# First chunk in halves, half of the attention output transposed by DMA, and a searched order, in a fused attention and gated feed-forward kernel

## The chip, the cores and the metric

The kernel runs on 1 core of a Trainium2 chip. The metric is the device time of one execution in microseconds (us). Every group of runs had the kernel before timed beside it on the same chip. A run is called slow when it is over 1.5% above the fastest of its kernel. "Profile" is one execution with the hardware profiler; its span is about 1.8 us shorter than the timed figure. "Granted clock" is the share of full speed that PE's clock had by the profile.

Engines: PE (matmul), DVE (vector), ACT (scalar), POOL and SP, which here mainly issue DMAs. Each engine works through its own list of instructions, in the order that the program fixed; semaphores join the lists. PE writes its results to banks of PSUM, and a bank must be read out by DVE or ACT before it is written again. In the profile's lines L1041 is line 1041 of the kernel file, SPq is SP issuing a DMA, and `ps` is a PSUM bank.

## The reference, cut to what matters

Four sequences of 768 tokens, 8 heads of 64. Heads 0, 2 and 6 see all earlier tokens, the others four sink tokens and a window of 64. The attention output, 3072 x 512, goes through a gated feed-forward block:

```python
x   = attention(q, k, v)                       # 3072 x 512
g   = x @ w_gate;  val = x @ w_val             # 512 -> 1536
ffn = (gelu(g) * val) @ w_out                  # 1536 -> 512
out = x + sigmoid(x @ w_res) * ffn
```

## The kernel before

It works in six chunks of 512 tokens, four tiles of 128 each. A builder in the kernel file writes tasks with priorities and assumed durations, simulates its own idea of the chip, and fixes the instruction list of every engine from it. The parts that the argument touches:

```python
P_ot = Pool(many("otile", 3, [128, D_MODEL], FP32))      # THREE output tiles
...
"gv": (4, one(6, 7, 5, 4, 3, 2))                         # four PSUM banks for gate and value results
...
# queries and keys, from the third chunk's loads on: transposed by DMA, issued from SP
t = G.add("sp", 1.3, ... dma_start(at(BB.qkt)..., sv(), transpose=True) ..., dma=0.6, name="dT")
...
# output of a chunk: four tiles
for lt in range(4):
    rb, sr, ot = Buf(P_ps, "out"), Buf(P_sr), Buf(P_ot)
    ...                                                  # 4 residual-gate and 12 output matmuls on PE
    t1 = G.add("dve", ..., "otile = (1 + tanh) * ffn", ..., name="gated")   # cut
    t2 = G.add("dve", ..., "otile += x", ..., name="add")                   # cut
    G.add("sp", 0.6, ... dma_start(out[r0:r0 + 128, w], at(ot)[:, w]) ..., dma=0.75, name="out")
...
for _ in range(360):                                     # blank matmuls where the builder sees PE idle,
    G.add("pe", 0.06, ... matmul(blank, blank) ..., 1e9, name="warm")       # until the first gate
```

A chunk has four output tiles and there are three buffers for them, so the fourth tile cannot be written by DVE before the first tile's store has landed. On SP the stores stand in one list with the transposes of queries and keys and with the copies of values that heads with a window need ("vs").

The softmax here doesn't subtract the row's maximum and nothing guards it: scores larger than these inputs give would overflow.

Of the kernel before, what the change touches and what calls it, by code (L numbers as in the profile page):

```python
# [36 lines left out]
ROWS_UNTIL = 2  # L37

VK = ((1, 4), (3, 4), (4, 5), (4, 7))

# [389 lines left out]
def build_kernel(nc, q, k, v, w_gate, w_val, w_out, w_res, out):  # L430
# [34 lines left out]
        "av1": (2, one(0, 1)), "av2": (1, [(0, 1)]), "av0": (3, [(0, 1), (6, 7), (2, 3)]),  # L465
        "sc": (2, [(2, 3), (4, 5)]), "scr": (3, one(5, 4, 3, 2)), "scr0": (3, one(6, 5, 4, 3, 2)),
        "gv": (4, one(6, 7, 5, 4, 3, 2)), "gv0": (4, one(6, 7, 5, 4)), "gv00": (2, one(6, 7)), "out": (2, one(6, 7)), "warm": (1, one(7, 5, 1)),
# [56 lines left out]
    def load_weights():  # L524
        for j in range(3):
            for nm, t, src in (("g", wg, w_gate), ("v", wv, w_val)):
                s = slice(j * 512, (j + 1) * 512)
                wtok[nm, j] = dma("pool", -20 + j, 2.6, (lambda t=t, s=s: lambda: t[:, :, s])(),
                                  src[:, s].rearrange("(ci p) f -> p ci f", p=128))
        wtok["r"] = dma("pool", -12, 2.6, lambda: wr[:, :, :], w_res.rearrange("(ci p) f -> p ci f", p=128))  # L530
        for j in range(4):
            s = slice(j * 3, (j + 1) * 3)
            wtok["o", j] = dma("pool", -11 + j, 1.95, (lambda s=s: lambda: wo[:, s, :])(),
                               w_out[j * 384:(j + 1) * 384, :].rearrange("(fi p) c -> p fi c", p=128))

# [14 lines left out]
    def values(b, a, z, base, each, on_engines=False):  # L550

        BB = batch(b)
        for i in range(a, z):
            BB.vtok[i] = dma("pool", base, 0.9, (lambda i=i: lambda: at(BB.v)[:, i, :, 0:DHEAD])(),
                             v[b, :, i * 128:(i + 1) * 128, :].rearrange("h p d -> p h d"), bufs=[BB.v])
            BB.vtok[i].late = 1.3
        if a == 0:

            def vk(on, j, h0, h1):
                def fn(e):  # L560
                    o = at(BB.vk)[32 * j:32 * j + N_SINK, 2 * j:2 * j + 2, :]
                    i_ = at(BB.v)[0:N_SINK, 0, h0:h1 + 1:h1 - h0, :]
                    return e.activation(out=o, in_=i_, func=AF.Copy) if on == "act" else e.tensor_copy(out=o, in_=i_)
                return fn
            BB.vktok = [G.flex({"dve": (0.3, vk("dve", j, *hs)), "act": (0.35, vk("act", j, *hs))},
                               [BB.vtok[0]], base + 1500, bufs=[BB.v, BB.vk], name="vk") for j, hs in enumerate(VK)]
            for t in BB.vktok:
                t.slack = 12.0 if b else 0.0
                if b == 0:
                    t.alts = {"dve": t.alts["dve"]}  # L570
        a_ = max(a, 1)
        if on_engines:
            ts = []
            for dst, src, off in ((0, 64, 1), (64, 0, 0)):
                def vs(on, dst=dst, src=src, off=off):
                    def fn(e):
                        o = at(BB.vs)[dst:dst + 64, a_ - 1:z - 1, :, :].rearrange("p i h d -> p (i h d)")
                        i_ = at(BB.v)[src:src + 64, a_ - off:z - off, :, :].rearrange("p i h d -> p (i h d)")
                        return e.activation(out=o, in_=i_, func=AF.Copy) if on == "act" else e.tensor_copy(out=o, in_=i_)
                    return fn  # L580
                n_ = (z - a_) * 520
                ts.append(G.flex({"dve": (c_dve(n_, 3.0, False), vs("dve")), "act": (c_act(n_), vs("act"))},
                                 [BB.vtok[i - off] for i in range(a_, z)], 130, bufs=[BB.v, BB.vs], name="vs"))
            for i in range(a_, z):
                BB.vstok[i] = ts
            late_copies.extend(ts)
            return
        cuts = range(a_, z) if each else [a_]
        for lo in cuts:
            hi = lo + 1 if each else z  # L590
            ts = []
            for dst, src, off in ((0, 64, 1), (64, 0, 0)):
                ts.append(G.add("sp", 1.2, (lambda lo=lo, hi=hi, dst=dst, src=src, off=off: lambda e: e.dma_start(
                    at(BB.vs)[dst:dst + 64, lo - 1:hi - 1, :, :].rearrange("p i h d -> p (i h d)"),
                    at(BB.v)[src:src + 64, lo - off:hi - off, :, :].rearrange("p i h d -> p (i h d)")))(),
                    [BB.vtok[i - off] for i in range(lo, hi)], base + 1, bufs=[BB.v, BB.vs], dma=0.15 * (hi - lo),
                    name="vs", grp=("vs", b, lo)))
            for i in range(lo, hi):
                BB.vstok[i] = ts

    def loads_rows(c, si, b, a, z):
# [18 lines left out]
        values(b, a, z, base + (10 if c == 0 else 8), False, c == 0)  # L620

        per = 1 if c == 0 or n == 4 else 2
        for k_ in range(0, NPAIR, per):
            ps_ = ORDER[k_:k_ + per]
            pr = 1000 * c - 492 + ps_[0] if c else 40 * k_ - 5
# [55 lines left out]
    def attention(c, segs, xbuf, xtbuf, xtoks, xttoks):  # L681
        tiles = [(b, i) for (b, a, z) in segs for i in range(a, z)]
        todo = []
        for k_, p in enumerate(ORDER):
            P = B()
            P.heads, P.p, P.c, P.pr = PAIRS[p], p, c, 1000 * c + 40 * k_
# [23 lines left out]
        sinks = sink_scores(c, [t for t in tiles if t[1] > 0], 1000 * c + 40 + 5)  # L710
        for t in ph(c, "sc")[:-1]:
# [11 lines left out]
        last, norms = None, []  # L723
        for P in todo:
# [3 lines left out]
            last, tn = weigh(P, tiles, sinks, xbuf, x16, xtoks, xdeps, last)  # L728
            if P.heads[0] % 2 == 1:
                for cb in (P.heads[0] // 2, P.heads[1] // 2):  # L730
                    to_features(c, cb, P.pr, x16, xdeps, xtbuf, xttoks)
# [5 lines left out]
            norms.append(tn)  # L737

# [87 lines left out]
    def sink_scores(c, need, pr):  # L826

        S = B()
        S.where, S.four, S.et = {}, {}, Buf(P_ek)
        scr = Buf(P_ps, "sc")  # L830
        for m, (b, i) in enumerate(need):
            for h in (1, 3, 5, 7):
                S.where[h, b, i] = m * 128
            S.where[4, b, i] = 512
# [3 lines left out]
        cols = (need + need[-1:])[0:4]  # L838
# [13 lines left out]
        for j, (b, i) in enumerate(cols):  # L852
            mms.append((j, batch(b), slice(0, 64), 1, 512, i * 128, 128))

        def sc(e):
# [7 lines left out]
        S.txs = [G.add("act", c_act(640), lambda e: e.activation(  # L863
            out=at(S.et)[:, 0:640], in_=at(scr)[:, 0:640], func=AF.Exp, scale=SM_SCALE),
            [ts], pr, bufs=[scr, S.et], fset="exp", name="expk")]
# [3 lines left out]
    def weigh(P, tiles, sinks, xbuf, x16, xtoks, xdeps, last):  # L869
        n = len(tiles)  # L870
        c, pr, heads = P.c, P.pr, P.heads
        av = Buf(P_ps, "av2" if c else "av0")
# [3 lines left out]
        def windows(xs, lts):  # L876
            def fn(e):
                r = []
                for x in xs:
                    for lt in lts:  # L880
                        b, i = tiles[lt]
                        o, w, BB, h = x * 512 + lt * 65, P.where[x, None, b, i], batch(b), heads[x]
                        for s in range(2):
# [3 lines left out]
                                              start=lt == 0, stop=(i == 0), skip_group_check=True))  # L887
# [3 lines left out]
        def keys(x, lt):  # L891
            def fn(e):
                b, i = tiles[lt]
                o = x * 512 + lt * 65
                return [e.matmul(at(av)[:, o:o + 65], lhsT=at(P.et)[:, P.where[x, kt, b, i]:P.where[x, kt, b, i] + 128],  # L895
                                 rhs=at(batch(b).v)[:, kt, heads[x], :], start=lt == 0 and kt == 0, stop=(kt == i),
# [3 lines left out]
        def sinkf(x, h):  # L900
            def fn(e):
                r = []
                for lt, (b, i) in enumerate(tiles):
                    if i == 0:
                        continue
                    o, ko = x * 512 + lt * 65, sinks.where[h, b, i]
# [25 lines left out]
        def avv(d0, d1):  # L932
            return at(av).rearrange("p (x w) -> p x w", x=2)[:, :, 0:n * 65].rearrange(
# [8 lines left out]
        xview = lambda: at(xbuf)[:, 0:n, :].rearrange("p i (y x d) -> p x i y d", x=2, d=128)[:, :, :, heads[0] // 4, half]  # L942
        direct = c == 0 or heads[0] % 2
        if direct:

            xdeps.append(G.add("dve", c_dve(2 * n * 64), lambda e: e.tensor_tensor(  # L946
                out=at(x16)[:, :, :, half], in0=avv(0, DHEAD), in1=scale(), op=ALU.mult), [t1], pr - 2.5, bufs=[av, rc, x16], name="norm16"))
        t2 = G.add("dve", c_dve(2 * n * 64), lambda e: e.tensor_tensor(  # L948
            out=xview(), in0=avv(0, DHEAD), in1=scale(), op=ALU.mult), [t1] + xdeps, pr - 2 + (200 if c == 0 and heads[0] else 0), bufs=[av, rc, xbuf], name="norm")
        for i in range(n):  # L950
            xtoks.setdefault(i, []).append(t2)
        if not direct:
            def cast(on):
                return lambda e: (e.activation(out=at(x16)[:, :, :, half], in_=xview(), func=AF.Copy) if on == "act" else
                                  e.tensor_copy(out=at(x16)[:, :, :, half], in_=xview()))
# [4 lines left out]
    def to_features(c, cb, pr, x16, xdeps, xtbuf, xttoks):  # L960
        n = 4
# [5 lines left out]
        def ev(on):  # L967
            def fn(e):
                o, i_ = at(xtbuf)[:, cb, 0:n * 128], at16(scr)[:, 0:n * 128]
# [7 lines left out]
    def gate_value(c, xtbuf, xttoks):  # L977
# [4 lines left out]
        for f in range(NF):  # L982
            pr = 1000 * c + 500 + f
            kind = "gv" if f > 1 else "gv0" if c or f else "gv00"
# [20 lines left out]
            toks.append(th)  # L1005
# [3 lines left out]
    def output(c, h, htoks, xbuf, xtoks, xtbuf, xttoks):  # L1009
        segs = [(b, t) for (b, a, z) in CHUNKS[c] for t in range(a, z)]  # L1010
        for lt in range(4):
# [14 lines left out]
            for w in ((slice(0, 256), slice(256, 512)) if last else (slice(0, 512),)):  # L1026
                fb = Buf(P_ps, "gv" if last else "out")
                n = w.stop - w.start
                for j in range(6):
# [3 lines left out]
                        [prev_t, wtok["o", j * 2 // 3], wtok["o", (2 * j + 1) // 3]] + htoks[2 * j:2 * j + 2], pr,  # L1033
# [22 lines left out]
    firsts = None  # L1056
    for t in late_copies:
        t.order += [x for d in (batches[0].ktok, batches[0].qtok) for (p, i), x in d.items() if i == 0]
    for c, segs in enumerate(CHUNKS):
        xbuf, xtbuf, xtoks, xttoks = Buf(P_x), Buf(P_xt), {}, []  # L1060
        attention(c, segs, xbuf, xtbuf, xtoks, xttoks)
        firsts = firsts or xttoks
        h, htoks = gate_value(c, xtbuf, xttoks)
# [3 lines left out]
    for c in range(len(CHUNKS)):  # L1067
        gv, gelu = ph(c, "gv"), ph(c, "gelu")
        for f, t in gv:
            t.order += ph(c, "sc") + (ph(c, "xT") if f > (1 if c else 0) else [])  # L1070
        for t in ph(c, "table"):
            t.order += ph(c, "exp") + ([x for _, x in firsts[:2]] if c == 0 else [])
# [6 lines left out]

    span = G.schedule()  # L1080
# [54 lines left out]
```

## Time and profile before

| | before |
|---|---|
| time, median (range), runs beside the change | 278.58 us (278.38 to 278.83, n = 4) |
| span in the profile, mean granted clock | 276.8 us, 1.00 |
| PE busy; idle after the opening | 98%; 1.4 us |
| landing of the first chunk's output stores | 6.6 to 7.4 us |

The lines that carry the bound are in the prediction. One view which I did not read before predicting matters most now: SP's own list between the first and the second chunk's output. The columns are start, time to the end of the group, what it issues, and how many.

```profile
52.77 0.38 SPq L1041 DMA_DIRECT2D out_dram<-otile  x1
...
56.86 13.20 SPq L669 DMA_TRANSPOSE qkt<-qks  x8
...
70.80 15.03 SPq L669 DMA_TRANSPOSE qkt<-qks  x8
85.87 1.64 SPq L1041 DMA_DIRECT2D out_dram<-otile  x3
```

The reader is to see that the first chunk's first store leaves at 52.77 and the other three only at 85.87, behind sixteen transposes whose issue takes 13.20 + 15.03 us. By DVE's list the data of these three were complete at 56.6, 63.3 and 66.5, so three of four stores already wait 20 to 29 us in this kernel. PE shows no wait from it (its longest after the opening is 0.7 us): the store that frees the buffer went ahead.

### The profile page before, as it was taken

Reading aid. Unit: us, or ns where it says so; the run is one execution under the profiler, and the core shown is the slowest. Engines: PE = TensorE matmul, PEld = TensorE weight load, DVE = VectorE, ACT = ScalarE, POOL = GpSimd, SP = SyncE. Lnnn points to the kernel's source line nnn. Section 1 sums busy time; section 2 is a strip of 40 time slices with the busy share of each in tenths; the row PEclk is TensorE's granted clock in tenths of the full one; section 3 lists DMA queues with packets and bytes.
Section 4 is the critical chain, followed back from the end, with each engine's and each line's share of the span. In section 5 each row is a group of like instructions: output and inputs, shape, how many; then the busy total and the mean of one; then the engine's idle time right before and its main releaser. Section 6 shows DMA issues by size and latency. Waiting matters only on the chain.

```text
span 276.8 us, 5687 instructions
## 1 busy us (share of the span) xinstructions
PE 270.3 (98%) x2407; PEld 138.9 (50%) x2407; DVE 143.0 (52%) x260; ACT 137.5 (50%) x199; POOL 86.2 (31%) x120
## 2 busy tenths in 40 slices
PE   7999999999899999999999999999999999999995
PEld 7775454455444456444455444456444455544443
DVE  2696342477433467534377533366633258633234
ACT  3655366673433966334773333766233777333210
POOL 8999249991491613991000000000000000000000
PEclk9999999999999999999999999999999999999999
DMA  6999999999999999999711100021100011200022
GB/s 88 165 203 207 185 206 177 151 194 133 176 131 154 247 138 201 158 155 125 191 41 73 44 0 2 0 76 41 40 0 0 2 41 38 78 2 0 0 76 78
DMA packets 92474, 27.81 MB, mean 100 GB/s; under 512 B 81184, under 2 KB 88864, under 8 KB 92448
## 3 DMA queue, kind: packets, MB, share of 16 engines
q0 software_dynamic: 70320, 14.69, 66.8%
q1 hardware_dynamic: 22128, 12.76, 23.7%
q8 instruction: 19, 0.31, 0.5%
q14 instruction: 7, 0.06, 0.1%
HBM read 29.36 MB, written 6.29 MB: 129 GB/s over the span
## 4 chain that ended last, share of the span: by engine, by line
PE 95%; DVE 2%; DMA 2%; issue 1%; ACT 0%; POOLq 0%
PE ps L988 45%; PE ps L1031 23%; PE ps L1016 7%; PE ps L768 5%; PE ps L895 3%; PE ps L1047 3%; PE ps L885 2%; PE ps L963 2%; PE ps L631 2%; DMA qks<-in_q_dram 2%; PE ps L909 1%; PE ps L856 1%; ACT xT L970 0%; DVE otile L1035 0%; DVE x L946 0%
## 5 line engine op out<-in xcount | busy, mean ns | idle before, releaser
L1002 DVE SCALAR_TENSOR_TENSOR hT<-gact,ps 128x512 f16<-128x512 f16 x72 | 49.5, 687 | 70.5 <-ACT gact L1000 70.5
L988 PE MATMUL ps<-xT,wg 128*128 128x512 f16 x288 | 85.2, 379 | 0.5 <-ACT xT L970 0.5
L988 PE MATMUL ps<-xT,wv 128*128 128x512 f16 x288 | 85.2, 379 | 0.0
L1000 ACT ACTIVATE gact<-ps 128x512 f16<-128x512 f32 x72 | 43.0, 597 | 78.2 <-PE ps L988 78.2
L1031 PE MATMUL ps<-wo,hT 128*128 128x512 f16 (+1 forms) x300 | 71.6, 371 | 0.2
L988 PEld LDWEIGHTS ps<-xT,wv 128*128 128x128 f16 x288 | 28.1, 98 | 33.8
L988 PEld LDWEIGHTS ps<-xT,wg 128*128 128x128 f16 x288 | 27.7, 98 | 33.7 <-ACT xT L970 0.6
L784 ACT ACTIVATE er<-ps 128x1024 f16<-128x1024 f32 (+3 forms) x40 | 34.5, 904 | 14.4 <-PE ps L768 14.4
L1031 PEld LDWEIGHTS ps<-wo,hT 128*128 128x128 f16 x300 | 25.8, 98 | 28.4 <-DVE otile L1035 3.7
L520 POOL DMA_DIRECT2D qks<-in_k_dram x36 | 28.4, 831 | 31.8 <-DMA qkt<-qks 22.8
L1035 DVE SCALAR_TENSOR_TENSOR otile<-srs,ps 128x512 f32<-128x512 f32 (+1 forms) x25 | 16.6, 664 | 26.4 <-PE ps L1031 26.4
L520 POOL DMA_DIRECT2D qks<-in_q_dram x36 | 28.9, 851 | 0.8 <-POOLq L1117 0.8
L1016 PE MATMUL ps<-wr,xT 128*128 128x512 f16 x96 | 24.7, 380 | 0.0
L520 POOL DMA_DIRECT2D va<-in_v_dram x24 | 21.4, 943 | 6.4 <-PE ps L909 6.4
L1019 ACT ACTIVATE srs<-ps 128x512 f32<-128x512 f32 x24 | 14.4, 598 | 12.4 <-PE ps L1016 12.0
L768 PE MATMUL ps<-qkt 64*128 64x64 f16 (+4 forms) x396 | 17.2, 215 | 0.0
L1038 DVE TENSOR_TENSOR otile<-otile,xtok 128x512 f32<-128x512 f32 (+1 forms) x25 | 16.5, 661 | 0.5
L948 DVE TENSOR_TENSOR xtok<-ps,rcp 128x512 f32<-128x512 f32 x24 | 16.3, 686 | 0.3
L768 PEld LDWEIGHTS ps<-qkt 64*128 64x128 f16 x396 | 10.3, 94 | 8.2 <-issue 3.4
L784 ACT ACTIVATE es<-ps 128x1024 f16<-128x1024 f32 x12 | 12.2, 1020 | 3.5 <-PE ps L768 3.5
L1016 PEld LDWEIGHTS ps<-wr,xT 128*128 128x128 f16 x96 | 8.7, 98 | 10.4 <-ACT gact L1000 0.5
L970 ACT ACTIVATE xT<-ps 128x512 f16<-128x512 f16 x11 | 6.3, 596 | 15.2 <-PE ps L963 15.2
(58 smaller groups left out, 197.0 us busy)
## 6 DMA issues: line engine op xcount, KB each, us to landing
out_dram<-otile SPq DMA_DIRECT2D x23, 256.0 KB, 2.5
va<-in_v_dram POOLq DMA_DIRECT2D x24, 128.0 KB, 17.7
qks<-in_k_dram POOLq DMA_DIRECT2D x32, 64.0 KB, 16.3
qks<-in_q_dram POOLq DMA_DIRECT2D x32, 64.0 KB, 16.9
wg<-in_moe_w_gate_dram POOLq DMA_DIRECT2D x3, 512.0 KB, 10.0
wv<-in_moe_w_val_dram POOLq DMA_DIRECT2D x3, 512.0 KB, 12.4
wo<-in_moe_w_out_dram POOLq DMA_DIRECT2D x4, 384.0 KB, 22.4
vs<-va SPq DMA_DIRECT2D x4, 260.0 KB, 5.8
```

What stands on the lines that cost most here:

```text
L520: return G.add(eng, issue, lambda e: e.dma_start(out_ap(), in_ap), deps, prio, bufs=bufs, dma=cost, name=name, grp=grp)
L768: return [e.matmul(at(scr)[:, oo:oo + w], lhsT=at(BB.qkt)[half, 1, p, k0:k0 + 128], rhs=at(BB.qkt)[half, 0, p, qq:qq + w], start=True, sto ...
L784: return e.activation(out=o, in_=i_, func=AF.Exp, scale=SM_SCALE)
L948: t2 = G.add("dve", c_dve(2 * n * 64), lambda e: e.tensor_tensor(out=xview(), in0=avv(0, DHEAD), in1=scale(), op=ALU.mult), [t1] + xdeps, ...
L988: return lambda e: [e.matmul(at(dst)[:, :], lhsT=w[:, ci, f * 128:(f + 1) * 128], rhs=at(xtbuf)[:, ci, :], start=(ci == 0), stop=(ci == NC ...
L1000: ta = G.add("act", c_act(512), (lambda gb=gb, ga=ga: lambda e: e.activation(out=at(ga)[:, :], in_=at(gb)[:, :], func=AF.Gelu))(), [tg], p ...
L1002: th = G.add("dve", c_dve(512), (lambda vb=vb, ga=ga, f=f: lambda e: e.scalar_tensor_tensor(out=at(h)[:, f, :], in0=at(ga)[:, :], scalar=0 ...
L1016: e.matmul(at(rb)[:, :], lhsT=at(xtbuf)[:, ci, s], rhs=wr[:, ci, :], start=(ci == 0), stop=(ci == NCB - 1))
L1019: ta = G.add("act", c_act(512), (lambda rb=rb, sr=sr: lambda e: e.activation(out=at(sr)[:, :], in_=at(rb)[:, :], func=AF.Tanh, scale=0.5)) ...
L1031: e.matmul(at(fb)[:, w], lhsT=at(h)[:, fi, s], rhs=wo[:, fi, w], start=(fi == 0), stop=(fi == NF - 1))
L1035: t1 = G.add("dve", c_dve(n), (lambda fb=fb, sr=sr, ot=ot, w=w: lambda e: e.scalar_tensor_tensor(out=at(ot)[:, w], in0=at(sr)[:, w], scala ...
L1038: t2 = G.add("dve", c_dve(n), (lambda ot=ot, lt=lt, w=w: lambda e: e.tensor_tensor(out=at(ot)[:, w], in0=at(ot)[:, w], in1=at(xbuf)[:, lt, ...
```

## The change

Its intent: let the first gate matmuls start when half of the first chunk's attention is done; take 32 transposes off PE from the third chunk on; and improve every engine's order by 137 searched priorities.

```diff
+DT_FIRST = 2
+HINTS = ("0:-35.76 3:-22.77 399:-347.39 ... 1675:7423.77 ")       # 137, cut
...
+            wtok["o", j].late = 2.2                               # allowance for the output weights
...
-        values(b, a, z, base + (10 if c == 0 else 8), False, c == 0)
+        values(b, a, z, base + (10 if c == 0 else 2), False, c == 0)
...
+                if (P.heads[0] < 4 and c >= DT_FIRST) or c >= DT_ALL:
+                    to_features_dma(c, P.heads[0] // 2, P.pr, x16, xdeps, xtbuf, xttoks)
+                else:
+                  for cb in (P.heads[0] // 2, P.heads[1] // 2):
+                    to_features(c, cb, P.pr, x16, xdeps, xtbuf, xttoks, l0, len(tiles))
...
+    def to_features_dma(c, cb, pr, x16, xdeps, xtbuf, xttoks):
+        t = G.add("sp", 1.3, lambda e: e.dma_start(
+            at(xtbuf)[:, cb:cb + 2, :]..., at(x16)[:, :, :, :]..., transpose=True), ..., dma=1.2, name="xD")
...
+            if f < len(halves) * 2:        # first four of the 12+12 slices of chunk 0: 256 columns per half
...
+        if c == 0:
+            for l0 in (0, 2):
+                last = attention(c, [(0, l0, l0 + 2)], xbuf, xtbuf, xtoks, halves[-1], l0, last, ek)
...
+    for x in "".join(HINTS).split():
+        n_, p_ = x.split(":")
+        G.tasks[int(n_)].prio = float(p_)
```

Cut: smaller forms of the same (masks, sinks and PSUM banks for two tiles, a copy of values in two pieces).

## The prediction

> **What bounds the kernel now.** I read the page's busy row and the chain of waits first, then a table of stages, then the chain piece by piece in the opening and at each place where it left the tensor engine (PE).
>
> ```profile
> PE 270.3 (98%) x2407; PEld 138.9 (50%) x2407; DVE 143.0 (52%) x260; ACT 137.5 (50%) x199; POOL 86.2 (31%) x120
> PE 95%; DVE 2%; DMA 2%; issue 1%; ACT 0%; POOLq 0%
> ```
>
> PE carries the span; DVE and ACT are half idle. But "busy" contains 151 matmuls on a blank tile that only keep PE occupied. The stage table (length, then PE, PEld, DVE, ACT, POOL busy) and the same table for the line of the blank matmuls:
>
> ```profile
> 0.00:5.66 5.66, 4.21 (x43) 4.04 (x44) 1.36 (x6) 1.49 (x2) 4.47 (x13) 1.00 0.53 65
> 5.66:22.62 16.96, 16.36 (x348) 13.16 (x349) 13.49 (x30) 10.75 (x15) 16.96 (x25) 1.00 1.52 187
> 22.62:273.70 251.08, 249.70 (x2018) 121.74 (x2018) 127.34 (x223) 125.23 (x183) 64.78 (x84) 1.00 0.89 96
> 273.70:276.80 3.10, 0.00 (x1) 0.00 (x0) 0.84 (x2) 0.00 (x0) 0.00 (x0) 1.00 0.25 85
> ...
> 5.66:22.62 16.96, 7.79 (x109) 6.16 (x109) 1.00 1.52 187
> ```
>
> So there are four stretches: waiting for the first load (5.66 us), a first-chunk attention of 16.96 us in which 109 blank matmuls sit, 251 us in which PE idles 1.4 us, and a 3.1 us tail. On the chain the blank matmuls of the second stretch add up to 7.0 us (0.83+0.67+0.78+0.50+0.27+0.62+0.28+0.50+1.35+1.18), plus 0.61 us of an ACT eviction: about 7.6 us without useful PE work. The last of it is where the first gate matmuls are waited for:
>
> ```profile
> 17.77 1.35 PE ps L1047 x21
> ...
> 20.34 0.61 ACT xT L970
> 20.95 0.05 issue
> 20.99 1.18 PE ps L1047 x18
> 22.17 0.45 PE ps L963 x8
> 22.62 0.55 PE ps L988 x2
> ```
>
> The reader is to see in it that gate and value (L988) wait for the whole 512-token attention, its transposes (L963) and their evictions (L970). After 22.62 the only real hole is in the second chunk:
>
> ```profile
> 68.62 0.70 DVE x L946
> 69.32 0.14 issue
> 69.45 0.40 PE ps L963 x4
> 69.85 0.02 issue
> 69.88 0.61 ACT xT L970
> ```
>
> PE's own timeline shows 0.69 us idle before the transposes and 0.47 us after them. The chain's DVE pieces at 141.7 to 145.0 are no hole: PE's timeline is filled there, with perhaps 0.4 us of slack.
>
> **What the Trainium skill says.** (1) "TensorE: Matmul & The Clock Gate", Part 4: PE-mode transpose: a transpose on PE lands in PSUM and needs a copy afterwards; it gives some 275 ns in a kernel. The trace has 219 ns for one, but 8 take 0.61 us, so the next starts after 56 ns; that spacing is what counts. The same page, Back-to-back issue gap, has N/2.4 + 2.5 ns per warm matmul. The trace agrees: 24 of 256 columns take 2.63 us on the chain, 110 ns each; 4 of 512 take 0.86, 216 ns each. So cutting 512 columns into two times 256 costs 4 ns. (2) "DMA: Bandwidth & Descriptors", DMA Transpose (X-bar): 2-byte data, destination SBUF, issued from the hardware queues. The kernel does this for queries and keys on SP: 1.28 us to issue, 2.5 to 9.0 us to landing. (3) "TensorEngine Tiling (Array Packing)", Key Properties: "Mode switching requires drain". Four residual-gate matmuls take 0.86 us, and 0.97 us after a tiled group: 0.11 us a switch. (4) "ScalarE: Activation LUTs", What ACT_TABLE_LOAD costs: 1283 ns for the load; the trace's loads mean 1283.
>
> **The change part by part.**
>
> *First chunk in halves.* Tiles 0-1, then 2-3; the first four of twelve gate/value slices are computed per half, 256 columns wide. The first half's four slices are 4 x 2 x 4 x 0.11 = 3.5 us of PE work that can run while the second half is in softmax. When can it start? The weights decide. Their issues and landings:
>
> ```profile
> L520 POOL DMA_DIRECT2D wg<-in_moe_w_gate_dram x3: 770/774/790, 10.6 to 13.6; - x3
> ...
> DMA to landing us min/median/max: 6.5/10.0/13.7
> L520 POOL DMA_DIRECT2D wv<-in_moe_w_val_dram x3: 760/780/799, 11.4 to 14.3; - x3
> ...
> DMA to landing us min/median/max: 8.2/12.4/15.4
> ```
>
> The first gate block lands at 10.6 + 6.5 = 17.1 us, the first value block at 11.4 + 8.2 = 19.6. What is wasted before 17.1 cannot be filled with them. After 17.1 the waste is 1.35 + 0.61 + 1.18 = 3.1 us: the ceiling of this part. Against it: DVE is busy most of the time from 10 us on, and halving adds instructions there (four more reciprocals at 0.20, four more normalisations at about 0.42 for half the width instead of 0.69, so 4 x (2 x 0.42 - 0.69) = 0.6, smaller masks, 0.5): about 2 us of DVE, and about 1.4 us of ACT exponentials. The second half is then ready about as late as the whole is now, 22 us, but PE has the first half's work. ACT's table load must follow all exponentials of both halves; four PSUM banks hold four results until then. I take 2.5 us of 3.1.
>
> *DMA transposes.* In chunks 3 to 6 feature blocks 0-1 go through one DMA per chunk. Removed: 4 x 8 = 32 transposes at 56 ns = 1.8 us of PE, and 8 evictions (0.42 on DVE or 0.60 on ACT, idle half the time: no gain). Moved: 4 DMAs of 256 KB on SP, about two of the present transposes each. The features are needed when the gate starts: in chunk 3 half of x is complete at 104.4 and the gates run densely from 112.4; in the others 146.3 to 153.3, 188.8 to 195.6 and 231.1 to 239.2. That leaves 7 to 8 us. Landings were 4.9 to 6.4 us around 104 to 108, and 2.5 to 4.5 us near 130 when loads thin out. Hidden in chunks 4 to 6, close in chunk 3. Gain 1.8 us on the bounding engine.
>
> *Order from a search.* About 150 priorities. What can it win? The hole of the second chunk, 0.69 + 0.47 = 1.2 us, of which I take 1.0. Mode switches: output matmuls hold 23.4% of 276.8 = 64.8 us of the chain, against 276 x 0.2157 + 24 x 0.110 = 62.2: 2.6 us, some 24 switches at 0.11; tiled groups pay again, perhaps 5 us in all. I take 1.0. Value loads of the second chunk also move ahead of the residual and output weights: the latter now land up to 21.6 + 24.2 = 45.8 us and are used first at 47.4. With gates earlier by 2.5 and weights later by four value loads of 128 KB (4 x 0.13 MB at the opening's 187 GB/s, 2.8 us) they meet.
>
> Sum: 2.5 + 1.8 + 1.0 + 1.0 = 6.3, less 0.9 for late landings and added switches of the halves: 5.4. 278.7 - 5.4 = 273.3; I say 273.4.
>
> **The rivals.** *A landing takes the place of the wait.* PE runs in order; a DMA transpose behind another on SP, or output weights landing near 48, would stop it. For: DMA is loaded until about 135 us, at 16 engines' full share in the page's row, and SP issues nine transposes from 104.6 to 121. Against: the slack computed above. It would return 1 to 3 us: 275 to 276.
> *DVE becomes the bound of the opening.* For: 13.49 of 16.96 us now, 2 us more after. If the second half is ready only at 24.5 us, gain is 3.5 + 22.6 - 24.5 = 1.6 us, not 2.5: 274.3.
> *The search finds more than I credit.* For: 7 us of switches, holes and slack exist. All of 3.1 + 1.8 + 1.6 + 2.5 = 9 us would be 269.7; I don't believe all of it.
> *Nothing is gained by DMA transposes because their PE slots were free.* Against: PE idles 1.4 us in 251. It would be 275.2.
>
> **Range and chances.** The parts are nearly independent, with errors of 0.8, 0.5, 1.5 and 1 us: about 2 us together. So 270.8 to 276.6 for 8 in 10. Faster by over 2% means below 273.2, next to my middle: 0.47. Within 2%: 0.51. Slower by over 2% needs stalls beyond 11 us, which nothing points to: 0.02.
>
> **What would show it.** Right: dense gate matmuls from about 20 us with no more than 1 us of blank matmuls or idle after 17.1; 32 fewer transposes on PE, with no PE wait on the four new DMAs; 0.2 us or less idle at the second chunk's transposes. Wrong: PE waits on value or output weights or a DMA transpose; a first full gate group later than 24 us; more 0.11 us surcharges than now.

## The result, and the profile after

| | before | after |
|---|---|---|
| time, median (range), n = 4 each | 278.58 us (278.38 to 278.83) | 283.60 us (283.17 to 283.88) |
| ratio, 95% interval | | 1.0178 (1.0161 to 1.0196) |
| span, clock in the profile | 276.8 us, 1.000 | 281.9 us, 0.982 |

A ratio is the mean time of one kernel's fast runs over that of the other's of the same rounds, so not quite the ratio of the medians. The change made the kernel 5 us slower. It is still within 2%, but well outside the predicted 270.8 to 276.6.

Where the time went is in the waits. The first line is from PE's waits of the changed kernel, the second from DVE's: total, times, longest.

```profile
PE ps L1054 <- DVE otile L1101: 8.1, 1, 8.1
```

```profile
DVE otile L1101 <- DMA out_dram<-otile: 10.5, 1, 10.5
```

Before, neither list had such a line: PE's longest wait was the 1.1 us for the blank tile. Now value matmuls (L1054) wait 8.1 us, once, for the line of DVE that writes an output tile (L1101). That line waits 10.5 us, once, for an output store to land. The chain of waits around it (start, length, what) and SP's list:

```profile
79.11 1.38 SPq L694
80.49 0.04 issue
80.54 6.54 DMA out_dram<-otile
87.08 0.02 issue
87.10 0.70 DVE otile L1101
87.80 0.05 issue
87.85 4.45 PE ps L1054 x10
```

```profile
55.95 24.54 SPq L694 DMA_TRANSPOSE qkt<-qks  x13
80.54 1.59 SPq L1107 DMA_DIRECT2D out_dram<-otile  x3
```

Against SP's list of before: there one store left at 52.77, ahead of the transposes. Here no store leaves until thirteen transposes are issued; their issue takes 24.54 us, 1.89 us each. The first store goes at 80.54 and lands 6.54 us later. DVE reaches the fourth output tile at 76.57, finds no free buffer and stops, and with it the products of gate and value that stand behind it in its list. These free the PSUM banks of the value results, so PE stops too, at about 79.7 us. The Trainium skill, page "DMA: Bandwidth & Descriptors", section Anatomy of one DMA, says that any semaphore wait happens on the issuing sequencer before dispatch. Such waits can hold a list, but here they did not: the chain shows the transposes' issues one after the other with 0.1 us or less between, so the store was held by the issue time of what stood before it.

The second part of the loss follows the wait. PE's timeline (start, length, instruction) and the windows (length; then busy time of PE, PEld, DVE, ACT, POOL; granted clock, DMA share, GB/s):

```profile
87.85 1.89 PE L1054 MATMUL ps<-xT,wv 128*128 128x512 f16 x4 [8.12 <-DVE otile L1101]
89.53 1.06 PE L1054 MATMUL ps<-xT,wg 128*128 128x512 f16 x2
```

```profile
60.00:80.00 20.00, 19.73 (x158) 9.57 (x155) 9.89 (x18) 9.22 (x16) 12.73 (x17) 1.00 1.78 136
80.00:88.50 8.50, 0.65 (x2) 0.28 (x3) 1.40 (x3) 0.36 (x1) 5.70 (x8) 0.64 1.61 213
88.50:92.70 4.20, 4.20 (x11) 1.49 (x10) 1.17 (x2) 0.37 (x1) 0.00 (x0) 0.52 1.83 194
92.70:115.00 22.30, 22.30 (x227) 10.91 (x225) 11.03 (x21) 15.64 (x22) 15.40 (x21) 1.00 1.66 151
```

After the idle time the clock stays at half until about 92.6 us: two 512-column matmuls start 0.85 us apart (89.53, 90.38, 91.23, 92.09), 425 ns each against 216. The twelve matmuls from 87.85 to 92.76 take 4.91 us instead of 12 x 0.216 = 2.6: 2.3 us are lost. The Trainium skill, "TensorE: Matmul & The Clock Gate", Part 1, names one idle window of about 3.4 us as enough for the half-rate state and about as long to leave it. In the trace, by windows of 0.2 us, the clock fell already 2.6 us after PE's last matmul (79.7 to 82.3), and it rose 4.7 us after the next one (87.85 to 92.6).

Idle and slow clock together are 8.12 + 2.3 = 10.4 us. The kernel lost 5. So some 5.4 us would have been won elsewhere, as much as the prediction promised, and a stall of 10.4 was laid on top. That is theory A. Its rivals are theory B, that the new DMA transposes or their landing cost the time, and theory C, that the opening in halves is itself slow.

### The profile page after: what moved, and what is told of

Same layout as the page of the kernel before. It is cut to its first block, busy times and chain, and to the rows that moved or that the text cites. A ratio compares the mean times of both kernels' runs of the same rounds, so it can differ in the third digit from the quotient of the medians.

```text
span 281.9 us, 5654 instructions
## 1 busy us (share of the span) xinstructions
PE 267.8 (95%) x2381; PEld 140.4 (50%) x2381; DVE 140.0 (50%) x272; ACT 141.2 (50%) x217; POOL 85.9 (30%) x120
## 4 chain that ended last, share of the span: by engine, by line
PE 68%; DMA 12%; POOL 9%; SPq 9%; issue 1%; DVE 1%; POOLq 0%
PE ps L1054 33%; PE ps L1097 19%; DMA va<-in_v_dram 9%; SPq L694 8%; PE ps L1082 6%; PE ps L800 4%; POOL va L543 3%; DMA out_dram<-otile 2%; POOL qks L543 2%; PE ps L933 2%; PE ps L923 1%; PE ps L947 1%; POOL wo L543 1%; POOL wv L543 1%; POOL wg L543 1%
## 5 line engine op out<-in xcount | busy, mean ns | idle before, releaser
L1054 PE MATMUL ps<-xT,wv 128*128 128x512 f16 x272 | 74.2, 386 | 8.1 <-DVE otile L1101 8.1
L1066 ACT ACTIVATE gact<-ps 128x512 f16<-128x512 f32 x68 | 40.5, 597 | 77.8 <-PE ps L1054 71.6
L1068 DVE SCALAR_TENSOR_TENSOR hT<-gact,ps 128x512 f16<-128x512 f16 x68 | 45.9, 687 | 63.6 <-PE ps L1054 40.5
L1054 PE MATMUL ps<-xT,wg 128*128 128x512 f16 x272 | 73.5, 383 | 0.0
L1097 PE MATMUL ps<-wo,hT 128*128 128x512 f16 (+1 forms) x300 | 69.9, 371 | 0.0
L1054 PEld LDWEIGHTS ps<-xT,wv 128*128 128x128 f16 x272 | 26.5, 99 | 40.0 <-DVE otile L1101 8.6
L1054 PEld LDWEIGHTS ps<-xT,wg 128*128 128x128 f16 x272 | 26.6, 99 | 31.0 <-issue 1.4
L816 ACT ACTIVATE er<-ps 128x1024 f16<-128x1024 f32 (+4 forms) x40 | 34.3, 891 | 10.4 <-PE ps L800 10.1
L1101 DVE SCALAR_TENSOR_TENSOR otile<-srs,ps 128x512 f32<-128x512 f32 (+1 forms) x25 | 16.5, 665 | 27.6 <-PE ps L1097 17.0
L1082 PE MATMUL ps<-wr,xT 128*128 128x512 f16 x96 | 24.4, 380 | 0.0
L986 DVE TENSOR_TENSOR xtok<-ps,rcp 128x512 f32<-128x512 f32 (+1 forms) x28 | 16.9, 607 | 0.4
L816 ACT ACTIVATE es<-ps 128x1024 f16<-128x1024 f32 (+1 forms) x14 | 12.6, 901 | 7.2 <-PE ps L800 7.0
L800 PEld LDWEIGHTS ps<-qkt 64*128 64x128 f16 x399 | 10.4, 94 | 9.8 <-issue 4.7
L1113 PE MATMUL ps<-blank 128*128 128x128 f16 x118 | 11.6, 247 | 2.6 <-DVE blank L517 2.6
```

The lines of the kernel that those rows point to most:

```text
L800: return [e.matmul(at(scr)[:, oo:oo + w], lhsT=at(BB.qkt)[half, 1, p, k0:k0 + 128], rhs=at(BB.qkt)[half, 0, p, qq:qq + w], start=True, sto ...
L816: return e.activation(out=o, in_=i_, func=AF.Exp, scale=SM_SCALE)
L986: t2 = G.add("dve", c_dve(2 * n * 64), lambda e: e.tensor_tensor(out=xview(), in0=avv(0, DHEAD), in1=scale(), op=ALU.mult), [t1] + xdeps, ...
L1054: return lambda e: [e.matmul(at(dst)[:, :], lhsT=w[:, ci, f * 128:(f + 1) * 128], rhs=at(xtbuf)[:, ci, :], start=(ci == 0), stop=(ci == NC ...
L1066: ta = G.add("act", c_act(512), (lambda gb=gb, ga=ga: lambda e: e.activation(out=at(ga)[:, :], in_=at(gb)[:, :], func=AF.Gelu))(), [tg], p ...
L1068: th = G.add("dve", c_dve(512), (lambda vb=vb, ga=ga, f=f: lambda e: e.scalar_tensor_tensor(out=at(h)[:, f, :], in0=at(ga)[:, :], scalar=0 ...
```

## The experiments

Sixteen runs. "After" below is the changed kernel. Where a task is moved, it is one instruction of one engine's list, and a comparison of the lists showed all other engines unchanged.

### 1. One store moved

```diff
+SP_MOVES = ((771, 455),)    # on SP: first output store, in front of two value copies and 13 transposes
-    span = G.schedule()
+    span = moved(G, G.schedule())
```

> The changed kernel with a single SP instruction moved: the first output store goes in front of the value copies and the 13 query/key transposes that stood before it; every other engine's order is the same. Theory A (the store is stuck in SP's order, so the third output tile is not freed, DVE stops at the fourth, PE stops 8.1 us and then runs some 5 us at half clock): both vanish, 283.6 - 8.1 - 2.3 = 273.2 us, between 272.3 and 275. Theory B (the new DMA transposes of the attention output, or their landing, cost the time): no gain from this, 283 +- 1. Theory C (the halved opening is what is slow): no gain either, 283 +- 1.

Measured: 274.09 us (273.38 to 275.92, n = 4), ratio 0.9837 (0.9792 to 0.9881); clock 1.0. SP's list and all of PE's waits:

```profile
56.97 0.39 SPq L1107 DMA_DIRECT2D out_dram<-otile  x1
...
58.63 23.40 SPq L694 DMA_TRANSPOSE qkt<-qks  x13
```

```profile
PE ps L1113 <- DVE blank L517: 2.6, 1, 2.6
PE ps L923 <- DVE er L852: 0.4, 1, 0.4
PE ps L947 <- DVE vk L587: 0.2, 1, 0.2
```

Here the store leaves as soon as DVE has finished its data (56.94). In "after" the same data were complete at 56.05, and the store left at 80.54, 24.5 us later. One instruction's place is worth 9.5 us, and the change without that fault gains 4.5 us. Theory A holds.

The converse on the kernel before, its first store moved behind sixteen transposes:

```diff
+SP_MOVES = ((717, 728),)    # on the kernel before
```

> The kernel before with its first output store moved behind the 16 query/key transposes that follow it on SP, nothing else. Theory A: the stall comes up in a kernel that has neither halves nor output transposes nor search. The store can go at about 85.4 us and lands 2.5 to 6.5 us later, DVE wants the fourth output tile at 65.1, so DVE waits over 20 us, PE 15 to 22 us, and the clock falls to half: 293 to 304 us. Theories B and C: nothing of theirs is in it, 278.6 +- 1.

Measured: 302.73 us (two runs, 300.95 and 304.52), ratio 1.0848 (1.0771 to 1.0926), clock 0.966.

```profile
PE ps L988 <- DVE otile L1035: 20.1, 1, 20.1
```

The same wait, in the old kernel with everything else as it was, 24 us slower. So the fault is neither of the halves nor of the transposes as such; it is the place of the store.

### 2. Which part brought it: the parts alone

Without the search and without DMA transposes (halves, with the smaller changes to value loads and weights):

```diff
-HINTS = ( ... )
+HINTS = ()
-DT_FIRST = 2
+DT_FIRST = 9
```

> The changed kernel without the priorities of the search and without the DMA transposes of the output: halves alone. The greedy order again puts 16 query/key transposes and both value copies in front of the first store on SP. Theory A: the stall is there without B's transposes, 283 to 296 us, with a PE wait on DVE's output tile of over 8 us. Theory B: without the transposes no stall, 277 to 279. Theory C: slow in the opening itself, first 512-wide gates later than 24 us, with no stall later, 280 to 283.

Measured: 290.92 us (289.60 to 292.20, n = 4), ratio 1.0425 (1.0383 to 1.0466), clock 0.981.

```profile
PE ps L1054 <- DVE otile L1101: 9.6, 1, 9.6
```

So the stall comes with the halves' part of the change: its tasks shift the builder's plan, and the store drops behind the transposes (which of this part's smaller changes shifts it was not separated). The same kernel with its first store moved as in experiment 1 shows what that part is worth without the stall:

> Halves alone (no search, no output transposes by DMA), with the first store in front on SP. As I predicted the halves they gain 2.5 us: 276.4. As the changed kernel's opening shows it (half of the first chunk's gates done at 33.2 us against 32.9 in the kernel before) they gain nothing because DVE is busy without a break from 13 to 28 us: 278.9, between 278 and 280.

Measured: 278.58 us (278.53 to 278.89, n = 4), ratio 0.9988 (0.9972 to 1.0003). The halves gain 0.3 us, within the noise, and not 2.5.

DMA transposes alone, put into the kernel before:

```diff
+                if P.heads[0] < 4 and c >= DT_FIRST:
+                    to_features_dma(c, P.heads[0] // 2, P.pr, x16, xdeps, xtbuf, xttoks)
+                else:                          # the rest as before
```

> The kernel before with the DMA transposes of half the output from the third chunk on, alone; the store keeps its place on SP. Theory A: 32 transposes of 56 ns leave PE, 276.8 us, between 276 and 278.3. Theory B: PE waits on them, 280 to 284. Theory C says nothing of it: 277 +- 1.

Measured: 278.45 us (277.96 to 279.32, n = 4), ratio 0.9982 (0.9958 to 1.0005), 0.5 us instead of 1.8. PE waits for the third chunk's transfer, which is issued at 106.63 behind two stores and a query or key transpose (in experiment 3 it leaves at 104.44, so its data were there):

```profile
PE ps L1000 <- DMA xT<-x: 1.1, 1, 1.1
```

Halves and DMA transposes without the search, store moved:

> Halves and DMA transposes in the greedy order (no search), with the first store in front. If the DMA transposes gain 0.5 us as they did alone and the halves nothing: 278.4, between 277.3 and 279.3, and the search is then what makes 274.1. If the parts are worth what I predicted (2.5 and 1.8): 274.6.

Measured: 277.65 us (276.73 to 278.86, n = 4), ratio 0.9954 (0.9922 to 0.9986): 1.3 us for both. Against the 0.9837 of experiment 1 and 0.9870 of its repetition below, the search is worth 0.84 to 1.17% of 278.8, 2.3 to 3.3 us, where 2.0 was predicted (each ratio is known to 0.3 to 0.4%).

Halves and search without DMA transposes, the searched priorities carried over to the same tasks:

```diff
-                    to_features_dma(...)
+                    to_features(... first block ...); to_features(... second block ...)   # back on PE
```

> Halves and search with the store in front, and the transposes of all chunks on PE again (each priority of the search still goes to the task it was found for; PE's order is the same up to the third chunk). If the 32 transposes cost PE's time in full, 274.1 + 1.8 = 275.9; if only what the DMA transposes brought alone, 274.6. Between 274.2 and 277.

Measured: 286.05 us (284.68 to 287.13, n = 4), ratio 1.0249 (1.0206 to 1.0292). PE waits 3.5 us in sum for DVE's output and 1.2 us for ACT's evictions, at many places, and the mean clock is 0.992. This does not measure the transposes: the searched order fits only the graph that it was searched for. Inconclusive.

### 3. The landing of the DMA transposes

The DMA-only kernel with the third chunk's transfer moved on SP in front of two stores and one query or key transpose:

```diff
+MOVES = (("sp", 977, 899),)    # on the DMA-only kernel
```

> The kernel before with the DMA transposes alone (which gave 278.45, ratio 0.998), and the third chunk's one moved on SP in front of two stores and one query/key transpose. Theory 'the DMA transposes' gain of 1.8 us was eaten by the 1.1 us wait for that landing, made by SP's order': the wait goes, 277.3 (ratio 0.994). Rival 'the freed PE slots were worth less than 56 ns each': 278.2 to 278.5, unchanged.

Measured: 277.98 us (277.32 to 278.81, n = 4), ratio 0.9971 (0.9948 to 0.9993). The wait of 1.1 us is gone from PE's list, the span of the profile is 275.6 against 276.8. The intervals of the two kernels overlap, so the timed difference alone settles nothing. The record's spans do: two of these four executions were timed 2.8 us above their span, where all others on record are 1.7 to 1.9 above it, so something outside the span is in the timed figure. The four spans are 275.4 to 276.0, all below the four of the DMA-only kernel (276.2 to 277.4). Against the kernel before beside each, the mean span is 0.5 us shorter with the wait and 1.4 without it (ratio 0.995, where 0.994 was expected). In the profiles the gain by the half-way point of chunks 3 to 6 grows 0.2, 0.5, 0.8, 1.2 us, 0.3 us a chunk, where 0.45 was predicted.

The same in the full change: experiment 1 again, and with the third chunk's transfer ahead of two query or key transposes.

```diff
-MOVES = (("sp", 771, 455),)                      # as SP_MOVES in experiment 1
+MOVES = (("sp", 771, 455), ("sp", 1031, 521))
```

> The changed kernel with its first output store in front of the waiting transposes, once more, as the partner for the next kernel. Both theories: 273.4 to 276 us, most near 274.0, with a spread between executions of up to 2 us.

> As the partner, but the third chunk's DMA transpose of attention output is issued in front of two query/key transposes on SP. Theory 'the late executions come from that transpose landing after PE needs it': issued about 2 us earlier it always lands in time; all executions within 0.5 us of each other, near 273.5 to 274.0, and no PE wait on it. Rival 'the spread has another source': the spread stays as it is (0.5 to 2 us), the middle within 0.3 us of the partner.

Measured: 274.62 us (274.13 to 276.87, n = 6), ratio 0.9870 (0.9836 to 0.9904), and 273.18 us (273.05 to 274.50, n = 5), ratio 0.9811 (0.9789 to 0.9832). The second is the best version found, and faster than both kernels. In its profile the transfer leaves at 101.78 and PE does not wait for it. Of four profiles with the order of experiment 1 on SP, PE did not wait in one (issued at 102.66), and waited 0.6, 1.5 and 2.0 us in the others (102.9 to 103.8). So the landing race is real. But the spread did not shrink to the expected 0.5 us (it is 1.45): of the 1.7 us between the two profiles, 0.86 us are gained in the opening, where the programs are the same. The same twelve blank matmuls, in the repetition of experiment 1 and then in the best version:

```profile
7.37 1.30 PE L1113 MATMUL ps<-blank 128*128 128x128 f16 x12
7.02 0.84 PE L1113 MATMUL ps<-blank 128*128 128x128 f16 x12
```

By the traces, blank matmuls start 107 ns apart until 8.4 us in the first and until 6.6 us in the second, and 56 ns apart from then on. So PE works 1.7 us longer at half rate, which costs about half of that, the 0.86 us. The column of the granted clock has 1.00 for both, so it does not show this. What sets the moment is open; in the traces of all runs it lies between 3.7 and 8.4 us, and differs between runs with the same opening.

### 4. Why the halves gave so little

The blank tile that the builder's warm-up matmuls read is cleared later under the searched order; PE waits 2.6 us for it instead of 1.1. Cleared first:

```diff
+MOVES = (("sp", 771, 455), ("dve", 0, 1))
```

> The changed kernel with the store in front, and with the clearing of the blank tile first on DVE again, as in the kernel before (the search had put it behind four others, so PE's blank matmuls begin at 2.6 us instead of 1.1, hold PE until 6.4 us while the first queries are there at 5.7, and the first 16 transposes still run slowly, 0.99 us instead of 0.57). If that delay of 0.8 + 0.4 us goes through the opening: 1.2 us under the version with the store alone (274.1), so 272.9, between 272.2 and 273.6. If DVE bounds the opening anyway: no more than 0.3 us.

Measured: 275.59, 275.74 and 274.34 us, and one slow run of 279.84 that is left out; ratio 0.9865 (0.9835 to 0.9895). In the one profile half of the first chunk's gate work was done at 34.12 us, as in experiment 1 (34.13): PE waited 2.2 us for the first loads instead. So the delay of the blank tile gained nothing when it was taken away.

DVE as the bound of the opening, the prediction's second rival: eight normalisations on DVE done twice.

```diff
-        t2 = ... e.tensor_tensor(out=xview(), in0=avv(0, DHEAD), in1=scale(), op=ALU.mult)
+        t2 = ... [e.tensor_tensor(out=spare(), ...)] if c == 0, then the same as before
```

> As the partner, but in the first chunk the eight float32 normalisations on DVE, which no PE work of the opening waits for, are done twice (the copy goes to a buffer that is not in use yet): eight more DVE instructions of about 0.34 us, five of them before 24 us. Theory 'DVE bounds the opening once the chunk is in halves': the second half's transposes (26.1 us at the latest) and all that follows come 1.5 to 2.7 us later: 275.5 to 276.7, and half of the first chunk's gate work is done at 35.6 to 36.8 instead of 34.1. Rival 'the halves gain nothing for another reason (weights' landings, PE's order)': under 0.5 us, 274 to 274.5.

Measured: 275.93 us (274.59 to 277.06, n = 4), ratio 0.9894 (0.9860 to 0.9927). The profiled run has 2.0 us of wait for the DMA transpose of experiment 3, so the total proves nothing. Half of the gate work was done at 33.21 us, not at 35.6 or later, so the theory did not hold as it was put. The opening can be read in the traces: the first gate matmuls with the doubled work, then the same of the best version.

```profile
21.23 0.60 PE L1039 MATMUL ps<-xT,wv 128*128 128x256 f16 x4
```

```profile
21.27 0.60 PE L1036 MATMUL ps<-xT,wv 128*128 128x256 f16 x4
```

That run's opening began earlier (its matmuls start 56 ns apart from 5.4 us on), so equal marks hide something: from the first normalisation of the fp16 output to the first gate it took 21.23 - 15.00 = 6.23 us against 21.27 - 15.88 = 5.39. Five profiles without the doubling agree on 5.38 to 5.39. Three instructions are doubled by then, 1.0 us, and they cost 0.84 us: DVE had hardly anything to spare there. From the first gate on, PE's timeline is the same to 0.05 us up to 32 us with five more doubled. So, by one profile with the doubling, DVE bounds the first half and not the second.

That left the blank matmuls: fixed filler on PE, in order, executed whether PE would have waited or not. Four kernels took them out, all behind the first real work or only those after about 12 us:

```diff
+    gone = set([t for t in G.prog["pe"] if t.name == "warm"][KEEP:])   # KEEP = 34, 43, 74, 87
+    ...                                   # out of PE's list; their dependencies handed on
```

> The changed kernel with both transfers moved, less the 84 blank matmuls that stand on PE after the first 34. Theory 'fixed filler holds the opening': each blank takes about 0.056 us of PE whether PE would have waited or not; the waits for DVE, ACT and loads that come in their place are shorter than the 4.7 us taken out: 271.0 to 272.5, gates from 19 to 20.5 us instead of 21.3. Rival 'the blanks only fill waits': 273.0 to 273.5, gates at 21.0 to 21.5, and waits of 4 us in sum appear on PE. A third possibility: the clock falls for want of work and the opening gets longer, 274 to 276.

> The kernel before, less the 108 blank matmuls that stand on PE after the first 43. Theory 'fixed filler': some gain here too, but less, as its gates wait for the whole chunk's attention: 277.5 to 278.3. Rival 'the blanks only fill waits': 278.6 to 279. Clock falls: 279.5 to 281.

> As the first, but only the 44 blanks after about 12 us are taken out, so the early ones still keep PE busy. Theory 'fixed filler': 271.3 to 272.7, nearly all of the first run's gain. Rival: 273.0 to 273.5.

> The kernel before, less only the 64 blanks after about 12 us. Theory 'fixed filler': 277.7 to 278.4, and the distance to the third run's kernel is 1 us or more larger than with the blanks in. Rival: 278.6 to 279.

| | blanks taken out | time, us (n = 4) | ratio, 95% interval | clock |
|---|---|---|---|---|
| best version | 84 | 275.20 | 0.9863 (0.9848 to 0.9878) | 0.975 |
| kernel before | 108 | 281.43 | 1.0084 (1.0063 to 1.0105) | 0.975 |
| best version | 44 | 275.28 | 0.9876 (0.9852 to 0.9900) | 0.987 |
| kernel before | 64 | 280.85 | 1.0068 (1.0032 to 1.0105) | 0.976 |

By the ratios, the four are 1.5, 2.3, 1.8 and 1.9 us slower than their partners (the best version was timed in another group): the third possibility, the clock. In the best version without any of the 84:

```profile
7.40:10.80 3.40, 2.25 (x52) 1.48 (x52) 2.40 (x5) 2.24 (x5) 3.40 (x9) 0.99 1.84 171
12.00:18.00 6.00, 4.49 (x72) 2.44 (x69) 5.81 (x19) 4.90 (x12) 6.00 (x8) 0.50 1.35 184
18.00:22.60 4.60, 4.12 (x58) 2.87 (x59) 3.44 (x13) 3.52 (x8) 4.60 (x7) 0.50 1.24 207
```

The clock falls at 10.75 us. In the 3.4 us before, PE was busy 66% of the time, and no gap was over 0.4 us. It then stays at half until 24.4 us, although PE, at half speed, is busy 75% and 90% of the two later windows. So the filler is not waste: it pays for the clock. The distance between the two kernels is 1.9% with the 44 and 64 blanks out, 2.2% with the 84 and 108 out, and 1.9% with all of them in, so the filler hid 0.3% of difference at most. "Fixed filler" as the cause fell, with the reservation that these runs differ in clock as well.

What can be read is the ledger of PE's opening, from the first real transpose to the moment when half of the first chunk's gate and value work is done. It is worked out from the traces, as the sum of the distances from one matmul's start to the next, so waits count with the instruction before them:

| us | before | halves, store moved | best version |
|---|---|---|---|
| first real transpose at | 5.66 | 5.67 | 6.38 |
| blanks and waits after them (blanks) | 7.10 (109) | 7.22 (94) | 6.69 (84) |
| attention and transposes | 9.81 | 10.71 | 9.74 |
| gate and value matmuls | 10.36 | 10.44 | 10.44 |
| half of the gate work done at | 32.93 | 34.04 | 33.25 |

The halves took 15 blanks out of the list and the time of blanks and waits did not fall; and the attention's own matmuls took longer. In that kernel, 0.7 + 0.5 us are waits for query and key loads, against 0.4 before, so chance of the loads is in it. The kernel without the search in experiment 2 has the same order on PE up to 105 us and no such waits; it reached the mark at 33.42. The halves then regain 1.07 us up to the same mark of the second chunk (79.21 against 79.17): the waits of 0.7 and 0.5 us at its transposes are absent there.

## Why the prediction was wrong

It said 273.4 us, and it was 283.6. Step by step:

**The sum had no term for stores.** This is the step that failed. The prediction took 0.9 us off "for late landings and added switches" and in its first rival asked whether a landing takes the place of a wait, naming the new DMA transposes and the output weights, at 1 to 3 us. It looked at what PE loads, not at what must leave before DVE can go on. The path that it missed runs from SP's list over the landing of the first store and the third output tile to DVE, and from DVE over the PSUM banks to PE. The runs put there a stall of 8.12 us idle and 2.3 us lost at half clock; the timed difference by moving one store is 9.5 us. "Slower needs stalls beyond 11 us, which nothing points to" was right in its sum (10.4 us against 5.4 won made 5 us of loss) and wrong in its reading: SP's list of before shows sixteen transposes, 28 us of issue, with three stores behind them, and three output tiles for four.

**Why the builder planned it so.** It counts 1.3 us for issuing a transpose and plans the store's landing for 76.5 us (from its own plan, no measurement), and puts DVE's fourth output tile right behind it, at 76.6. DVE came there at 76.57 on the chip too, but the chip takes 1.89 us for each of thirteen transposes, 7.6 us more in sum, and 6.54 us for the landing. That the search was run on that plan, and so could not see the stall, is argued from this and not tested.

**Halves, +2.5.** Wrong by about 2.2: 0.3 in the run with the store moved. The signs named were dense gates from about 20 us and a first full group before 24. Gates began at 21.3 to 22.2 in this order, 0.4 to 1.3 us earlier than before instead of 2.5, while the second half's attention still had to be done among them; its last transposes came at 26.2 to 27.1, against 22.3 for the whole chunk before, and later than even the rival's 24.5. The prediction let the weights' landing (17.1 and 19.6) decide when gates can start and expected the second half at 22; the ceiling of 3.1 us was read as time that gate work could fill. But the first half is ready only shortly before the whole chunk was. The rival "DVE becomes the bound" is half right: it holds for the first half and not for the second. A clean split of the missing 2.2 us is open.

**DMA transposes, +1.8.** Right in kind, too large in size: 0.5 us with the landing wait in the third chunk; without it 0.8 timed, 1.2 in the profile and 1.4 in the mean span. "Close in chunk 3" was right: 0.6 to 2.0 us of wait there in three of four profiles with the store moved.

**Search, +2.0.** It was 2.3 to 3.3. The second chunk's hole is gone, as predicted, though the halves alone also close it. PE changes its tiling form 84 times after 36 us instead of 91, 0.8 us at the prediction's 0.11 us. The rest is not assigned.

**The sum of gains.** 5.4 was predicted; with the store moved it is 4.5 us (3.6 in the repetition), and with the transpose moved too the ratio 0.9811 gives 5.3 us and a median of 273.18. That agreement is partly luck: the halves were over- and the search underestimated.

## What to carry to other kernels

Before trusting a new order, list for each issuing engine what stands in front of every store, and compare the number of buffers with the number of results in flight: a transfer that frees a buffer belongs ahead of transfers that only prefetch. When a model chose the order, compare its assumed issue and landing times with the trace first; a plan that is exact to 0.1 us in the model has no slack on the chip. And when a change that should help makes a kernel slower, look for one long wait and move that one instruction before giving up its parts.

## What the Trainium skill lacked or had wrong

- "DMA: Bandwidth & Descriptors", Issuing engines are not separate DMA queues, calls the sequencer time saved by several issuing engines "usually small relative to the DMA itself". For one DMA that holds here (a query or key transpose: 1.35 us to issue against 7.1 us to landing, medians of the changed kernel). The section does not say that issue times add up in a list: thirteen transposes held SP's sequencer for 24.54 us, and the store behind them cost 9.5 us of kernel time, 24 us in the converse experiment.
- The same page, DMA Transpose (X-bar), gives no issue times (elsewhere the page has a bandwidth, and cycle counts in a table for another chip generation). Here a query or key transpose took 1.65 to 1.89 us of issue in a row, and a 256 KB one of attention output 1.23 to 2.79 us.
- The same page, Anatomy of one DMA, has about 2.0 us of fixed cost (for DMAs issued from GpSimd), and says elsewhere that it grows with load, without a figure for a whole store. The 256 KB output stores, issued from SP, took 6.5 to 7.4 us to land while loads were under way; the median of all of them is 2.3 to 2.5 us.
- "TensorE: Matmul & The Clock Gate", HAM oscillation, states the rule as no idle gaps of PE over about 3.4 us. Here the clock fell 2.6 us after PE stopped, and in the kernel without 84 blanks it fell with PE busy 66% of 3.4 us and no gap over 0.4 us; the page's next section mentions frequent short idling, without a share at which it begins.
- No page says that blank matmuls in the gaps pay for themselves by the clock: taking out 44 to 108 of them cost 1.5 to 2.3 us in each of four kernels.
